# A hand-written order of single-engine steps, extended over all eight attention units and a second weight chunk

## The chip, the cores and the metric

The kernel runs on one core of a Trainium2 chip. The metric is device time in microseconds (us) of one execution. A core has a matrix engine (TensorE, "PE" in profile rows; its weight loads are "PEld"), VectorE ("DVE"), ScalarE ("ACT"), GpSimd ("POOL") and SyncE ("SP"), which issues most of the transfers. Each engine runs its own instructions in the order in which they stand and waits for the others by semaphores. That order is settled when the program is built.

## The reference

Attention with 32 packed queries per head, then two feed-forward layers over 2,304 tokens, all in float32:

```python
def sm_attn(qq, kk, vv):                        # scale = 1/8
    s = scale * np.matmul(qq, kk.transpose(0, 1, 3, 2))
    a = np.exp(s - np.max(s, axis=-1, keepdims=True))
    a = a / (np.sum(a, axis=-1, keepdims=True) + 1e-09)
    return np.matmul(a, vv)
p_packed = sm_attn(p, k, v)                     # q, k, v: 4 x 8 x 576 x 64, p: 4 x 8 x 32 x 64
x = sm_attn(q, p_packed, p_packed)              # then 2304 x 512
h = x @ w_in                                    # 512 x 2048
x = (np.maximum(h, 0) + np.log1p(np.exp(-np.abs(h)))) @ w_out
out = (1 / (1 + np.exp(-(x @ w_gate))) * (x @ w_val)) @ w_out2      # 512 x 1536, 1536 x 512
```

## The kernel before

**Attention** is cut into eight units `u = 2b + g`: batch `b` (of 4), a group `g` of four heads. The steps of a unit, each on one engine (class `Unit`; the two letters are their names in the list below):

- `lk`, `lq`, `lv`: SP loads k, q or v of the unit, 576 KB each, into a *place*. Places 0 to 5 are sixths of the tile `xa`, which later takes the first layer's output (batches 0 and 1 in 0 to 2, batches 2 and 3 in 3 to 5); place 6 is a tile of its own. A load into a place waits until what stood there has been read. `PLACE` (L216) gives the places of k, q and v of each unit.
- `kx`, `qx`: GpSimd (suffix p, L112) or ScalarE (a, L406) copies half of k or q into another order (tile `x`, two buffers); `kt`, `qt`: three transposes on TensorE (L416); `kc`, `qc`: ScalarE (a) or VectorE (d) takes them out of PSUM (L104, L106). `tp`, `cp`: the same for p (L384, L391).
- `sc` (L440): scores on TensorE; `mx`, `ex`, `nm`: maximum, exponential, division (VectorE, ScalarE, VectorE); `wt`, `wc`: the weights transposed (L472) and taken out; `va` (L492): the product with v, after which v's place is free; `pk`: the packed values into the tile `bdT`; `sp`: their split into two parts.
- `ss` (L521): the second scores, in two halves of the 576 tokens; `sb` (VectorE, L534 and L535), `ee` (ScalarE, L541), `sm` (VectorE, L545 to L547), `ml` (GpSimd, L551): their softmax; `tn` (L572): three transposes on TensorE; `hh`, `hl`: the result split into two parts, `A2h` and `A2l`.

**The first layer** goes by batch `b`, by chunk `c` of 256 of the 2,048 columns of `w_in`, and by half `s` of the tokens. `ri`, `ro` load raw weights (two buffers), `ci`, `co` convert them in three VectorE steps each, `oh`, `ol` split `w_out`. `wp` (L708) multiplies the packed values with `w_in`, `wh` and `wl` split the product; `hp` (L121 to L123, 12 matmuls) multiplies it with the attention weights; `ha` (three ScalarE steps), `hg` (VectorE), `gh` (ScalarE or GpSimd) and `gl` (GpSimd, L109) make the activation and split it; an `op` (L864, L865, L867, six matmuls) is a quarter `m` of the product with `w_out`, and `oc` adds it into `xa`. **The second layer** follows; the change doesn't touch it.

**The order.** `first_part` (L1075) walks through `SCRIPT` (L1047), a list of 371 words. Each word issues one of the steps; the digits are unit, head pair and half, or batch, chunk, half and quarter. `*n` puts n filler matmuls (L371) ahead of the step; there are 102 of them in all. While it runs, `held` keeps every engine's instructions in the order of the words. The list covers units 0 to 4 (`NU = 5`) and chunk 0 of batches 0 and 1. A loop over `entries` (batch, chunk) does the rest: for each it emits `hp` and the activation of this entry and the `op` of an earlier one, and between quarters it advances a queue of weight work (`jobs`) and, by a pace worked out from what is left, the attention units 5 to 7 (`attn_unit`, up to three alive at a time). Instructions of the loop are put in order by the tile framework's scheduler when the program is built.

```python
        for m in range(KD):
            take_out1(b, c, s, m, product_out1(c, m, g), CP0)
            between(m, att_ticks)
```

Of the kernel before, what the change touches and what calls it, by code (L numbers as in the profile page):

```python
# [21 lines left out]
def attn_moe_moe_kernel(  # L22
# [182 lines left out]
    def convert_split(key, pool, shape, tag, bufs):  # L205
# [61 lines left out]
    jobs = deque()  # L267
# [87 lines left out]
    E1 = nc.scalar  # L355
    WARM = 0
    BEHIND = []
    NU = 5
    FOUR = 3
    SPC = 2  # L360

# [660 lines left out]
    def prep_B(ps, f):  # L1022
# [22 lines left out]


    SCRIPT = """  # L1047
        lk0 lk1 lq0 lv0 lq1 lv1 tp0 cp0 kx00p tp1*7 kx01a cp1 lk2 kt000*12 kt001 ri00 kc000a
        kt010 kc001d kt011 kc010d kc011a kx10p tp2*5 sc0 kx11p kt100 mx0 cp2 kt101 kt110 kc100a
        qx01p kt111 kc110a kc101d ex0 kc111d qt010*10 qt011 sc1 qc010a nm0 qc011a qx00a mx1 wt01  # L1050
        wt00 lq2 qt000 wc00a wc01d qt001 ex1 qc000d va0*4 qx10p qc001a nm1 qx11p qt101 pk0a lv2
        qt100 qc101d qt110 ri01 sp0 ss01 qc100d lk3 qc110d wt10 sb01 ss00 wc10a qt111 ee01 sb00
        wt11 kx20p tp3 qc111a wc11a kx21p sm01 kt201*10 cp3 kt200 va1 ee00 ml01 ci000 kc200a
        ci001 kc201a kt211 pk1a kt210 sm00 tn01 kc211a sp1 ss10 kc210a ci002 qx20a sc2 ml00 sb10
        ro00 hh01 lq3 qt200 qx21p tn00 hl01 ee10 mx2 ss11*5 hh00 lv3 qc200a sm10 ex2 qt211 qt210
        hl00 qc211a ml10 sb11 qc210a qt201*12 qc201a ci010 tn10*11 ee11 nm2 hh10 kx31p tp4*7 cp4
        hl10 wt21*8 kx30p kt310 ci011 wc21a kt311 wt20 kc310a kt301 ci012 kc311a kt300 kc301a
        co000 ro01 wp00 kc300a sm11 wc20a sc3 wh00 co001 qx30p va2 qx31p mx3 ml11 co002 ex3
        qt301 lk4 qt311 wl00 oh00p lq4 pk2a lv4 qc311a nm3 tn11*11 sp2 ri10 ss20 qc301a hh11
        co010 wt30 ol00 sb20 wt31 wc30a hp000 wc31a hl11 ee20 co011 va3 ha000 sm20 qt310 co012  # L1060
        ml20 ss21 pk3a hg000 ri11 qc310a tn20 sp3 wp10 oh01a sb21 hh20 ss31 ol01 wh10 hl20 ee21
        wl10 qt300 hp001 kx40a kx41p sb31 qc300a gh000p sm21 kt401 ee31 kt411 gl000 kc401a ss30
        ci100 ha001 kc411d kt400 op0000 sb30 qx40p op0001 ml21 oc0000a hg001 op0003 kc400a
        oc0001d ee30 gh001p qt400 ci110 kt410 oc0003a qt401 ci111 qx41p qc400a op0002 kc410a
        sm30 gl001 tn21 qc401a qt410 oc0002a qt411 sc4 hh21 ci112 ml30 qc410a qc411a hl21 op0011
        sm31 tn30 oc0011a op0012 hh30 mx4 ml31 op0013 oc0012a hl30 ex4 op0010 ci101 tn31 oc0013a
        hp100 ci102 oc0010a hh31 nm4 ro10 wp01 ro11 ha100 hl31 wt41 wt40 wc41d hp101 wc40d wh01
        hg100 va4 wl01 ha101 gh100p co100 gl100 co101 hp010 pk4a co102 op1001 hg101 oh10p ha010
        op1000 co110 ol10 co111 ss41 gh101p co112 oc1001a op1003 oc1000a gl101 hg010 oh11a ss40
        oc1003a sb41 op1002 ol11 gh010a hp011 sb40 ee41 gl010 oc1002a sm41 ee40 op1013 ha011  # L1070
        sm40 ml41 op1011 op1012 oc1013d ml40 oc1011a op1010 hg011 sp4 oc1012a tn41 gh011a
        oc1010d tn40 hh40 gl011 hh41 hl40 hl41
    """

    def first_part():  # L1075
# [14 lines left out]
        for word in SCRIPT.split():  # L1090
# [18 lines left out]
            elif do in ("lk", "lq", "lv"):  # L1109
                assert place[do[1], at[0]] not in busy  # L1110
                load_one(do[1], at[0], place[do[1], at[0]])
            elif do in ("ri", "ro"):
                assert waiting[0] == ({"ri": "in", "ro": "out"}[do], *at)
                load_next()
            elif do == "ci":
                c, f, _ = at
                if (c, f) not in part:
                    if f == 0 or c not in w_in_f:
                        w_in_f[c] = ph1.tile([P, KD, CF], F32, tag="w_in", bufs=2, name="w_in")
                    part[c, f] = convert(("in", c, f), w_in_f[c][:, :, f * P : (f + 1) * P])  # L1120
                next(part[c, f], None)
            elif do == "co":
                if at[:2] not in raw_cv:
                    raw_cv[at[:2]] = new_cv()
                    part["o", *at[:2]] = convert(("out", *at[:2]), raw_cv[at[:2]])
                next(part["o", *at[:2]], None)
            elif do == "oh":
                wo_hl[at] = [
                    wo_p.tile([P, DM], F32R, tag="wo" + y, bufs=4, name="wo" + y) for y in "hl"
                ]  # L1130
                hi_of(eng != "p", wo_hl[at][0], raw_cv[at])
            elif do == "ol":
# [279 lines left out]
```

## Time and profile before

| | before |
|---|---|
| three runs | 858.75, 863.81, 864.49 us (median 863.81) |
| profiled execution | 858.43 us, of which the span from first to last instruction is 856.6 us |
| TensorE busy | 833.8 us, 97% of the span |
| VectorE, ScalarE, GpSimd busy | 595.9, 333.1, 497.6 us |
| mean granted TensorE clock | 0.998 |

In the profile "busy" counts instructions from start to modelled end, and matmuls overlap, so the time lost is better seen in the idle time ahead of an instruction and in what ended it. The clock column gives the share of full speed that was granted.

### The profile page before, as it was taken

The page shows a single profiled execution, that of the slowest core. Times are in us where ns is not written, and L with a number is a line of the kernel's source. Part 1 is how long each engine was busy: PE and PEld are TensorE (multiplying, and loading weights), DVE is VectorE, ACT ScalarE, POOL GpSimd, SP SyncE. Part 2 cuts the span into 40 slices and gives each one's busy share as a digit, 9 for nine tenths or more (in the row PEclk, how much of TensorE's full clock was granted, in tenths as well). Part 3 has the DMA queues.
Part 4 walks back from the last instruction along what each step waited for, and adds up shares of the span by engine and source line. Part 5 has one row for each costly group of instructions (what it writes and reads, how often), then busy time and mean ns, then how long its engine had stood idle before and what let it go on. Part 6 is the DMA issues. An engine that isn't in the chain of part 4 may idle for free.

```text
span 856.6 us, 15955 instructions
## 1 busy us (share of the span) xinstructions
PE 833.8 (97%) x6218; PEld 777.9 (91%) x6218; DVE 595.9 (70%) x1003; ACT 333.1 (39%) x615; POOL 497.6 (58%) x497
## 2 busy tenths in 40 slices
PE   9899989999999999999999999999999999999997
PEld 6789879999999999999999999999988999999995
DVE  4799456946746375458898688897896656766665
ACT  4677656554433334434324422232442432322210
POOL 4485434245857474693679787796892733536400
PEclk9999999999999999999999999999999999999999
DMA  9983330304453233500164464544414412213003
GB/s 230 219 219 103 84 84 2 99 1 121 128 152 106 69 99 99 154 2 1 42 194 152 138 192 151 168 140 155 142 56 142 125 44 80 68 44 111 14 1 111
DMA packets 61868, 90.83 MB, mean 106 GB/s; under 512 B 7648, under 2 KB 40544, under 8 KB 61792
## 3 DMA queue, kind: packets, MB, share of 16 engines
q1 hardware_dynamic: 60784, 88.56, 36.8%
q10 hardware_dynamic: 1008, 1.25, 0.4%
q8 instruction: 49, 0.80, 0.4%
q14 instruction: 27, 0.22, 0.1%
HBM read 65.67 MB, written 18.87 MB: 99 GB/s over the span
## 4 chain that ended last, share of the span: by engine, by line
PE 42%; DVE 5%; DMA 1%; issue 1%; ACT 1%; POOL 0%; DVEq 0%; ACTq 0%
PE bank L123 9%; PE bank L121 9%; PE bank L122 9%; PE ps L1327 5%; PE ps L1328 5%; PE ps L1329 5%; DVE aop L109 1%; DMA raw_v<-in_moe_w_val_dram 1%; DVE bank L1280 1%; DVE work L1280 1%; DVE work L1292 0%; DVE xa L1335 0%; DVE xa L903 0%; DVE sum L903 0%; ACT aop L929 0%
## 5 line engine op out<-in xcount | busy, mean ns | idle before, releaser
L121 PE MATMUL bank<-aop,BH 128*128 128x288 f32 x672 | 199.1, 296 | 3.7 <-DVE work L1292 0.9
L123 PE MATMUL bank<-aop,BL 128*128 128x288 f32 x672 | 198.6, 296 | 0.0
L122 PE MATMUL bank<-aop,BH 128*128 128x288 f32 x672 | 197.8, 294 | 0.2 <-DVE aop L109 0.2
L875 DVE TENSOR_TENSOR xa<-xa,ps 128x288 f32<-128x288 f32 x224 | 99.5, 451 | 101.0 <-PE ps L867 100.8
L109 POOL TENSOR_TENSOR ghl<-g,ghl 128x576 fp32r<-128x576 f32 x64 | 93.4, 1463 | 101.4 <-ACT ghl L116 76.6
L864 PE MATMUL ps<-ghl,woh 128*128 128x288 f32 x512 | 146.4, 301 | 3.2 <-DVE xa L875 2.2
L865 PE MATMUL ps<-ghl,wol 128*128 128x288 f32 x512 | 143.5, 295 | 0.0
L121 PEld LDWEIGHTS bank<-aop,BH 128*128 128x128 f32 x672 | 126.2, 188 | 9.6 <-POOL BL L109 1.1
L122 PEld LDWEIGHTS bank<-aop,BH 128*128 128x128 f32 x672 | 126.4, 188 | 4.1 <-DVE aop L109 0.4
L123 PEld LDWEIGHTS bank<-aop,BL 128*128 128x128 f32 x672 | 126.5, 188 | 0.0
L109 POOL TENSOR_TENSOR BL<-cv,BH 128x512 fp32r<-128x512 f32 (+1 forms) x96 | 117.3, 1237 | 3.4 <-ACT BH L116 2.4
L867 PE MATMUL ps<-ghl,woh 128*128 128x288 f32 x512 | 109.3, 295 | 0.1
L864 PEld LDWEIGHTS ps<-ghl,woh 128*128 128x128 f32 x512 | 96.1, 188 | 6.7 <-DVE xa L875 3.2
L865 PEld LDWEIGHTS ps<-ghl,wol 128*128 128x128 f32 x512 | 96.3, 188 | 0.1
L1280 DVE TENSOR_TENSOR work<-work,bank 128x576 f32<-128x576 f32 (+1 forms) x100 | 70.8, 725 | 31.1 <-PE bank L123 31.0
L1327 PE MATMUL ps<-oh,gv 128*128 128x512 f32 x216 | 84.5, 391 | 1.0 <-DVE xa L1335 0.6
L1328 PE MATMUL ps<-ol,gv 128*128 128x512 f32 x216 | 84.9, 393 | 0.0
L1329 PE MATMUL ps<-oh,gv 128*128 128x512 f32 x216 | 84.8, 393 | 0.0
L867 PEld LDWEIGHTS ps<-ghl,woh 128*128 128x128 f32 x512 | 82.3, 188 | 0.7 <-POOL ghl L109 0.6
L112 POOL TENSOR_SCALAR BH<-cv 128x512 fp32r<-128x512 f32 (+1 forms) x48 | 30.1, 638 | 89.0 <-PE bank L122 88.8
L1335 DVE TENSOR_TENSOR xa<-xa,ps 128x512 f32<-128x512 f32 x90 | 61.6, 684 | 28.2 <-PE ps L1329 27.9
L121 PE MATMUL ps<-A2h,wph 128*128 128x288 f32 x256 | 76.6, 299 | 0.1
(151 smaller groups left out, 1645.1 us busy)
## 6 DMA issues: line engine op xcount, KB each, us to landing
cv<-B SPq DMA_DIRECT2D x52, 256.0 KB, 2.7
B<-cv SPq DMA_DIRECT2D x48, 256.0 KB, 3.6
raw_in<-in_moe_w_in_dram SPq DMA_DIRECT2D x16, 512.0 KB, 3.9
raw_out<-in_moe_w_out_dram SPq DMA_DIRECT2D x16, 512.0 KB, 3.6
raw_g<-in_moe_w_gate_dram SPq DMA_DIRECT2D x12, 512.0 KB, 3.9
raw_v<-in_moe_w_val_dram SPq DMA_DIRECT2D x12, 512.0 KB, 4.3
raw_o<-in_moe_w_out_dram SPq DMA_DIRECT2D x12, 512.0 KB, 4.2
xs<-cv SPq DMA_DIRECT2D x56, 64.0 KB, 2.0
```

The costliest lines, as they stand in the source:

```text
L109: hold(eng.tensor_tensor(lo, x, hi.bitcast(F32), op=ALU.subtract))
L121: hold(nc.tensor.matmul(ps, wh, xh, start=first, stop=False))
L122: hold(nc.tensor.matmul(ps, wh, xl, start=False, stop=False))
L123: hold(nc.tensor.matmul(ps, wl, xh, start=False, stop=last))
L864: hold(nc.tensor.matmul(out_, wh[:, ms], gh[:, f], start=f == 0, stop=False))
L865: hold(nc.tensor.matmul(out_, wl[:, ms], gh[:, f], start=False, stop=False))
L867: hold(nc.tensor.matmul(out_, wo_hl[c, f][0][:, ms], gl[:, f], start=False, stop=f == 1))
L875: hold(nc.vector.tensor_tensor(dst, dst, out_, op=ALU.add))
L1280: nc.vector.tensor_tensor(to, x, y, op=ALU.add)
L1327: nc.tensor.matmul(bank, gh[:, ts_], oh, start=f == 0, stop=False)
L1328: nc.tensor.matmul(bank, gh[:, ts_], ol, start=False, stop=False)
L1329: nc.tensor.matmul(bank, gl[:, ts_], oh, start=False, stop=f == 1)
```

## The change

`SCRIPT` grows from 371 to 585 words. It goes on over units 5 to 7 and over chunk 0 of batch 2 (up to its activation) and chunk 1 of batches 0 and 1, and it is arranged anew from its first line on; the number of fillers stays 102. `NU` is 8, so no unit is left to the loop, and the loop begins two entries later. Units 6 and 7 get places of their own. Some copies change engines: in the stretch that differs VectorE has nine instructions more, ScalarE seven and GpSimd two fewer. No operation of the computation is added or removed. From unit 7's last transposes (`tn`) on, TensorE's instructions stand in the same order in both kernels to the end; ahead of it they are the same ones in another order.

```diff
     PLACE = {
         0: "345", 1: "621", 2: "345", 3: "634", 4: "563", 5: "456",
-        6: "565", 7: "656",
+        6: "345", 7: "634",
     }
...
-    NU = 5
+    NU = 8
...
     SCRIPT = """
-        lk0 lk1 lq0 lv0 lq1 lv1 tp0 cp0 kx00p tp1*7 kx01a cp1 lk2 kt000*12 kt001 ri00 kc000a
+        lk0 lk1 lq0 lv0 lq1 lv1 tp0 cp0 kx00p kx01a kt010*24 lk2 kt000 ri00 kc010d kt001 kc000a
...
-        oc1010d tn40 hh40 gl011 hh41 hl40 hl41
+        hl40 tn41 qt510 oc0113 hh41 va5 kx60p kx61a hl41 qc510a kt611 pk5a lk7 kt610 kc611d
+        kt601 lq7 sp5 kc610a ss50 kc601d qx60a op0100 sb50 kt600 op0101 qx61p kc600a oc0100 ee50
...
+        tn71 hh61 hl70 hh71 hl61 hl71
     """
...
             elif do == "ci":
                 c, f, _ = at
                 if (c, f) not in part:
-                    if f == 0 or c not in w_in_f:
+                    if c not in w_in_f:
...
-        for b, c in ((0, 0), (1, 0)):
+        for b, c in ((0, 0), (1, 0), (0, 1), (1, 1)):
             for s in range(2):
                 gt.pop((b, c, s))
...
-    jobs.append(("wp11", prep_wp_one(1, 1)))
+    jobs.append(("wp21", prep_wp_one(2, 1)))
...
-    pend.extend((0, 1, s) for s in range(2))
+    pend.extend((2, 0, s) for s in range(2))
     for i, (b, c) in enumerate(entries):
-        if i < 3:
+        if i < 5:
             continue
```

What this does to the engines' orders, at two places. The first is TensorE around unit 5's second softmax. Before, the loop's order has unit 6's scores (`L440`) and four groups of k or q transposes, then both of unit 5's `tn` (`L572`, reading its tiles `a2`) and two `wp`:

```order
L440 MATMUL ps2_1676<-kT_1574,pT0_109 64x288 x4
L416 MATMUL ps1_1695<-ident_101,x_1693 128x96 x3
L416 MATMUL ps1_1701<-ident_101,x_1693 128x96 x3
L416 MATMUL ps1_1708<-ident_101,x_1706 128x96 x3
L416 MATMUL ps1_1713<-ident_101,x_1706 128x96 x3
L572 MATMUL ps1_1720<-ident_101,a2_1644 128x96 x3
L572 MATMUL ps1_1726<-ident_101,a2_1660 128x96 x3
L708 MATMUL ps1_1732<-w_in_462,bdT_106 64x256 x4
L708 MATMUL ps1_1741<-w_in_947,bdT_106 64x256 x4
L121 MATMUL ps2_1750<-A2h2_116,wph_1737 128x288
```

In the changed kernel the first of the two (`tn50`) stands behind a `wp` and the first transposes of unit 7's k (`kt711`, `kt710`):

```order
L708 MATMUL ps1_1632<-w_in_466,bdT_106 64x256 x4
L416 MATMUL ps1_1640<-ident_101,x_1630 128x96 x3
L416 MATMUL ps1_1647<-ident_101,x_1630 128x96 x3
L572 MATMUL ps1_1651<-ident_101,a2_1577 128x96 x3
L440 MATMUL ps2_1657<-kT_1547,pT0_109 64x288 x4
L416 MATMUL ps1_1665<-ident_101,x_1638 128x96 x3
L121 MATMUL ps2_1674<-A2h2_116,wph_1644 128x288
```

and the second (`tn51`) comes 47 rows later, behind an `hp` (its last row stands first here) and unit 6's `ss61`, with `va7` and unit 6's first `tn` after it:

```order
L123 MATMUL ps2_1832<-A2h1_115,wpl_1814 128x288
L521 MATMUL ps1_1850<-bdT_106,qT_1606 96x64 x6
L572 MATMUL ps1_1864<-ident_101,a2_1724 128x96 x3
L492 MATMUL ps1_1868<-a1T_1827,xa_78 64x32 x24
L572 MATMUL ps1_1902<-ident_101,a2_1846 128x96 x3
L416 MATMUL ps1_1906<-ident_101,x_1699 128x96 x3
```

So the two `tn` of the unit no longer stand together, and each has other products ahead of it. The second place is SP's queue with the loads of the last units. Before, chunk 2's raw weights are followed by k6, v6, q6, k7, v7, q7 (those named `xa_78` are in a place of `xa`):

```order
L165 DMA raw_in_1382<-in_moe_w_in_dram 128x4x256
L165 DMA raw_in_1384<-in_moe_w_in_dram 128x4x256
L252 DMA xa_78<-in_k_dram 96x4x384
L252 DMA xa_78<-in_v_dram 96x4x384
L252 DMA q6_1606<-in_q_dram 96x4x384
L252 DMA k7_1718<-in_k_dram 96x4x384
L252 DMA v7_1864<-in_v_dram 96x4x384
L252 DMA xa_78<-in_q_dram 96x4x384
```

In the changed kernel k6, p7, q6 and v6 stand ahead of those weights, and k7, q7, v7 behind them:

```order
L252 DMA xa_78<-in_k_dram 96x4x384
L311 DMA p_1257<-in_p_dram 128x64 x2
L252 DMA xa_78<-in_q_dram 96x4x384
L252 DMA xa_78<-in_v_dram 96x4x384
L165 DMA raw_in_2085<-in_moe_w_in_dram 128x4x256
L165 DMA raw_in_2087<-in_moe_w_in_dram 128x4x256
L252 DMA k7_1541<-in_k_dram 96x4x384
L252 DMA xa_78<-in_q_dram 96x4x384
L252 DMA xa_78<-in_v_dram 96x4x384
```

The three loads of unit 7 now follow one another, and k7 is the one in place 6.

## Rows read from the trace of the kernel before

**Rows 1.** The page's first part: busy us (share) xinstructions.

```profile
span 856.6 us, 15955 instructions
PE 833.8 (97%) x6218; PEld 777.9 (91%) x6218; DVE 595.9 (70%) x1003; ACT 333.1 (39%) x615; POOL 497.6 (58%) x497
```

**Rows 2.** Busy time by stretch: from:to, length, each engine's busy us, granted clock, DMA share, GB/s.

```profile
1.50:45.00 43.50, 39.64 (x488) 31.69 (x489) 26.16 (x64) 23.45 (x64) 20.61 (x32) 1.00 1.01 235
45.00:60.00 15.00, 15.00 (x173) 14.04 (x172) 13.95 (x26) 12.23 (x27) 11.39 (x16) 1.00 0.95 234
60.00:90.00 30.00, 28.77 (x263) 26.05 (x262) 25.84 (x47) 19.02 (x41) 18.91 (x20) 1.00 0.32 93
90.00:120.00 30.00, 26.88 (x244) 22.08 (x243) 15.05 (x34) 17.79 (x44) 12.08 (x16) 0.94 0.40 100
120.00:151.00 31.00, 29.93 (x322) 28.06 (x321) 18.65 (x46) 18.09 (x43) 11.67 (x17) 1.00 0.08 21
0.00:151.00 151.00, 140.28 (x1480) 121.97 (x1481) 100.13 (x216) 91.35 (x218) 75.61 (x106) 0.99 0.55 134
151.00:857.00 706.00, 693.49 (x4740) 655.96 (x4738) 495.75 (x787) 241.76 (x399) 421.99 (x391) 1.00 0.34 100
```

**Rows 3.** TensorE's timeline: start, us, what, count [idle before <-what ended it].

```profile
35.58 0.30 PE L384 MATMUL ps<-ident,p 128*128 128x128 f32 x1 [2.44 <-DMA p<-in_p_dram]
...
42.33 0.47 PE L416 MATMUL ps<-ident,x 96*128 96x96 f32 x3 [0.56 <-POOL x L112]
42.63 0.78 PE L371 MATMUL ps<-hot 128*128 128x128 bf16 x11
...
64.02 0.47 PE L572 MATMUL ps<-ident,a 96*128 96x96 f32 x3 [1.18 <-POOL a L551]
...
109.17 1.51 PE L416 MATMUL ps<-ident,x 96*128 96x96 f32 x12 [0.17 <-POOL x L112]
111.75 0.47 PE L572 MATMUL ps<-ident,a 96*128 96x96 f32 x3 [1.07 <-POOL a L551]
113.00 0.74 PE L572 MATMUL ps<-ident,a 96*128 96x96 f32 x3 [0.79 <-POOL a L551]
...
150.17 0.47 PE L572 MATMUL ps<-ident,a 96*128 96x96 f32 x3 [0.85 <-POOL a L551]
```

**Rows 4.** TensorE's timeline, sixteen `wp` instructions at two places.

```profile
113.68 3.25 PE L708 MATMUL ps<-w_in,bdT 128*64 128x256 f32 x16
...
151.38 1.95 PE L708 MATMUL ps<-w_in,bdT 128*64 128x256 f32 x16
```

**Rows 5.** GpSimd's timeline, the copies of unit 3's k.

```profile
35.11 1.63 POOL L112 TENSOR_SCALAR x<-k 96x768 f32<-96x768 f32 x2 [3.86 <-DMA k<-in_k_dram]
```

**Rows 6.** Timelines of TensorE and GpSimd: unit 5's second scores and softmax multiplies.

```profile
104.86 2.18 PE L521 MATMUL ps<-bdT,qT 128*96 128x64 f32 x24
...
110.86 0.83 POOL L551 TENSOR_TENSOR a<-a,m 96x384 f32<-96x384 f32 x1 [0.96 <-ACT qT L104]
112.12 0.83 POOL L551 TENSOR_TENSOR a<-a,m 96x384 f32<-96x384 f32 x1 [0.43 <-ACT a L456]
```

**Rows 7.** Loads of k1, k3, k7 (tile `k`) to landing; ScalarE's copies of k or q.

```profile
DMA to landing us min/median/max: 4.4/5.7/16.0
...
L406 ACT ACTIVATE x<-xa 96x768 f32<-96x768 f32 x4 | 3.4, 840 | 0.4 <-DMA xa<-in_q_dram 0.4
```

**Rows 8.** TensorE's timeline: the first matmuls of two `op` that follow each other.

```profile
82.18 0.29 PE L864 MATMUL ps<-ghl,woh 128*128 128x288 f32 x1
...
82.99 0.29 PE L864 MATMUL ps<-ghl,woh 128*128 128x288 f32 x1
```

**Rows 9.** Groups by line in 0:151: VectorE's copies of k's transposes (busy us, mean ns).

```profile
L106 DVE COPY kT<-ps 128x288 f32<-128x288 f32 x5 | 2.1, 451 | 7.4 <-PE ps L416 7.4
```

**Rows 10.** Waits in 0:151: total us, times, longest.

```profile
PE ps L572 <- POOL a L551: 3.9, 4, 1.2
```

More of the change, by code (lines that the diff above doesn't have):

```diff
@@ L1047, in attn_moe_moe_kernel @@
     SCRIPT = """
-        lk0 lk1 lq0 lv0 lq1 lv1 tp0 cp0 kx00p tp1*7 kx01a cp1 lk2 kt000*12 kt001 ri00 kc000a
[L1049 to L1070, printed above, removed]
@@ L1071, in attn_moe_moe_kernel @@
-        sm40 ml41 op1011 op1012 oc1013d ml40 oc1011a op1010 hg011 sp4 oc1012a tn41 gh011a
-        oc1010d tn40 hh40 gl011 hh41 hl40 hl41
+        lk0 lk1 lq0 lv0 lq1 lv1 tp0 cp0 kx00p kx01a kt010*24 lk2 kt000 ri00 kc010d kt001 kc000a
+        kt011 kc001d tp1 kc011a kx10p cp1 sc0 kx11p tp2 kt100 mx0 cp2 kt101 kt111 kc100a kt110
+        qx01p kc101d ex0 kc110d qx00p qt010*12 kc111a nm0 qt011 sc1 qc011a lq2 qc010d wt01 mx1
+        wt00 wc01a qt000 qt001 wc00a ex1 va0*6 qx11p qc001a nm1 qx10p qc000a qt110 pk0a lv2
@@ new lines, in attn_moe_moe_kernel @@
+        qt111 ri01 qt100 qc110a sp0 qc111d ss01 lk3 qc100d wt11 sb01 ss00 wc11a wt10 ee01 sb00
+        qt101 kx20p wc10a qc101a va1*9 sm01 kx21p ee00 sm00 ml01 kt200 pk1a kt210 ci000 tn01
+        kc200a sp1 kt201 ci001 kc210a kt211 kc201a ss10 ci002 kc211a qx21p hh01 sc2 sb10 ro00
+        ml00 lq3 hl01 ee10 qx20p mx2 qt210*11 tn00 qc210a lv3 qt200 sm10 hh00 tp3 qt201 ex2 hl00
+        ml10 ci010 cp3 ss11*14 ci011 qc200a qc201a tn10 qt211 nm2 hh10 qc211a sb11 wt20*13 kx30p
+        kx31a hl10 wc20a kt300*13 ci012 ee11 kt311 tp4 kt310 kc300a co000 ro01 kc311a wt21 sm11
@@ new lines, in attn_moe_moe_kernel @@
+        cp4 kt301 kc310a wp00 kc301a co001 ml11 wc21a sc3 qx30a co002 qx31p va2 wh00 mx3 oh00a
+        wl00 ex3 ol00 qt311 lk4 qt310 pk2d tn11 lq4 qc311a nm3 ss21 lv4 sp2 hh11 ri10 qc310a
+        qt300 hl11 wt31 sb21 qc300a wt30 hp000 wc31a wc30a co010 ee21 co011 va3 ha000 sm21 co012
+        ml21 tp5 ss20 pk3a hg000 ri11 cp5 sp3 tn21 lk5 wp10 oh01a sb20 hh21 ss30 ol01 wh10 hl21
+        ee20 wl10 qt301 hp001 qx40p kx40a sb30 qc301a gh000p sm20 ee30 qt401 gl000 kt401 qc401a
+        qt400 kt400 kc401d ha001 ss31 kc400d qx41p qc400d op0002 sb31 kx41p qt411 oc0002a op0001
@@ new lines, in attn_moe_moe_kernel @@
+        hg001 ml20 qc411a op0000 ee31 ci110 gh001p oc0001a kt411 ci111 op0003 oc0000a gl001
+        kc411a ci112 kt410 oc0003a qt410 tn20 kc410a sm31 kx51p op0012 qc410a hh20 op0011 sm30
+        ml31 oc0012a kx50a tp6 sc4 hl20 ml30 oc0011a ci100 kt501 ci101 cp6 op0013 kc501a mx4
+        kt500 oc0013a tn30 op0010 hh30 kc500d ex4 hl30 kt511 tn31 ci102 hp100 hh31 oc0010a nm4
+        ro10 kc511a ro11 wp01 lq5 ha100 hl31 lv5 wt41 wt40 wc41d kt510 hp101 kc510d wh01 hg100
+        wc40a wl01 gh100p sc5 ha101 co100 gl100 co101 va4 mx5 op1003 pk4a lk6 hg101 lq6 ex5
@@ new lines, in attn_moe_moe_kernel @@
+        op1002 sp4 co110 co111 ss40 oc1003a qx51p qx50a co112 hp011 oc1002a lv6 sb40 oh11p qt511
+        gh101p ha011 op1000 nm5 gl101 qt500 qt501 co102 hp010 qc511a qc501d oh10p oc1000a hg011
+        qc500a op1011 ol10 ha010 op1013 oc1011d ol11 wt50 oc1013d tp7 op1010 wc50d cp7 ss41
+        hg010 gh011a oc1010a gl011 op1012 sb41 ee40 wt51 oc1012a op1001 sm40 ee41 op0110 gh010p
+        wc51a sm41 oc1001a op0111 ml40 op0112 oc0110 ml41 oc0111 tn40 oc0112 op0113 gl010 hh40
+        hl40 tn41 qt510 oc0113 hh41 va5 kx60p kx61a hl41 qc510a kt611 pk5a lk7 kt610 kc611d
@@ new lines, in attn_moe_moe_kernel @@
+        kt601 lq7 sp5 kc610a ss50 kc601d qx60a op0100 sb50 kt600 op0101 qx61p kc600a oc0100 ee50
+        qt601 oc0101 qt600 lv7 qc601a qt611 sm50 qt610 qc600a op0102 qc610a qc611d ml50 kx71a
+        wp20 oc0102 kx70p kt711 wh20 kt710 tn50 qx71p sc6 wl20 hh50 hl50 kt700 kc710a mx6 hp200
+        kc700a kc711a ex6 kt701 qt710 qx70p kc701a ss51 nm6 ha200 sc7 qc710d sb51 wt60 wt61
+        wc60a qt701 mx7 qt711 wc61a op0103 qc701a hg200 va6 ex7 oc0103 gh200p qc711a nm7 gl200
+        ee51 wp11 pk6a sm51 wt70 sp6 wh11 wt71 ss60 wc70a wl11 wc71a ml51 hp111 sb60 ee60 ss61
@@ L1073, in attn_moe_moe_kernel @@
+        ha111 sm60 tn51 va7 sb61 ml60 hh51 hg111 ee61 tn60 qt700 hl51 pk7a hp110 qc700d gh111a
+        sp7 sm61 hh60 ss70 ha110 hl60 ml61 ss71 sb70 gl111 hp201 hg110 ee70 sm70 gh110a op1111
+        ha201 sb71 ml70 op1112 op1110 gl110 oc1111 oc1112 op1113 ee71 hg201 op1101 oc1110 gh201p
+        op1100 oc1113 gl201 sm71 op1102 oc1101 op1103 ml71 oc1100 tn70 oc1102 tn61 hh70 oc1103
+        tn71 hh61 hl70 hh71 hl61 hl71
     """
```

## The prediction

> **What bounds the kernel now.** I read the page's first part, then busy time by stretch, then TensorE's timeline with the idle time ahead of each row. The page says TensorE is busy 97% of the span [rows 1]; the other engines matter only where TensorE waits for them. The order shows where the change can act: from the piece `tn71` (unit 7's last turning, 150.17 us in the trace [rows 3]) to the end, TensorE has the same instructions in the same order in both kernels, and ahead of it the same instructions, 102 fillers among them, in another order. So the stretch 0 to 151 us is in play and the 706 us behind it are not. In 0:151 TensorE is idle 151.00 − 140.28 = 10.72 us [rows 2]. By stage: 3.86 in 1.5:45, nothing in 45:60, 1.23 in 60:90, 3.12 in 90:120 and 1.07 in 120:151 [rows 2]; the rest is the first 1.5 us.
>
> The list of before ends with unit 4's last pieces, ahead of the stretch 90:120; from there on the loop interleaves units 5 to 7. So the list's own stretch from 45 to 90 loses 1.23 us and the loop's from 90 to 151 loses 4.19. The clock comes on top: in 90:120 the granted clock is 0.94 on average [rows 2], all else being 1.00, so TensorE dropped to its lower level (1.2 of 2.4 GHz) for a while. What it did before: twelve transposes, a wait of 1.07 us, three transposes, a wait of 0.79, three transposes [rows 3]. The same sixteen `L708` products then took 3.25 us, and 1.95 at full clock [rows 4]: 1.3 us lost at least; 0.06 of 30 us is 1.8 at most. I take 1.5.
>
> **The change part by part.**
>
> *The late waits (removed).* Two of the three largest waits of 90:151 are unit 5's turnings `tn` and the third is unit 7's, all for the GpSimd multiply that ends the softmax [rows 3]. In before both halves of unit 5's second product run back to back (104.86 to 107.04) and the multiplies end at 110.86 + 0.83 = 111.69 and 112.95 [rows 6]: the chain needs 4.7 us for the first half and 5.9 for the second. The loop put too little between. In after's order, behind `ss50` stand three `op`, seven transposing words and a `wp` ahead of `tn50`: 3 × 0.81 [rows 8] + 7 × 0.38 (1.51 / 4 for three transposes [rows 3]) + 1.95 / 2 [rows 4] = 6.1 us, against 4.7. Behind `ss51` stand a whole `hp` (12 matmuls of 0.81 / 6, 1.6 us), two `ss` (2.18 [rows 6]), two transposing words (0.76), a `va` and four `wt` ahead of `tn51`: 4.5 us before the last two kinds are counted, and the half runs alone, so 4.7 is its chain. Behind `ss71` stand an `hp` and eight `op`, 1.6 + 6.5 = 8.1 us, against 5.9. So I expect these waits gone, and with them the clock's fall: 4.19 + 1.5 = **5.7 us**. Bounds: 3.1 (only the three waits that I traced, 1.07 + 0.79 + 0.85, and 0.4 of the rest) and 4.19 + 1.8 = 6.0.
>
> *The start (rearranged).* Unit 3's k arrives when the loads let it: its first copy on GpSimd begins at 35.11, the moment of landing [rows 5], since the queue is full (DMA share 1.01 up to 45 us [rows 2]). SP's queue is the same in both orders up to unit 5's k, so I leave that time alone. Before waits 2.44 us at `tp4` [rows 3] and afterwards still runs 19 of its 102 fillers; after has run all 102 by then, and one `wt` more, but has `tp4` yet to do. Eleven fillers take 0.78 us at most [rows 3], so 19 are up to 1.35 us that after has spent inside an unavoidable wait; some of before's lie inside waits too (eight while the copy finishes). I take **0.95**; bounds 0 and 1.7 (19 fillers and a `wt`, three transposes, of 0.38).
>
> *Unit 7's own places (added).* k7 goes to place 6, which v5 holds until `va5` has read it; q7 follows in place 3, v7 in 4. k7's load is issued behind `va5`, and TensorE wants the copy of k7 at `kt711`. Between stand eight transposing words, an `ss` and three `op`: 8 × 0.38 + 1.09 + 3 × 0.81 = 6.6 us, less where a row's end lies beside the next one's start; I take 5.4. The load takes 4.4 us with an empty queue [rows 7] and the ACT copy 0.84 [rows 7], 5.4 with handovers: a wait of 0 to 0.8, **0.3** taken. Everything behind `kt711` on TensorE waits with it. Ahead of k7 on SP stand two weight loads (chunk 2) that wait for `co102`; an `hp`, nine `op` (1.6 + 7.3 us) and small pieces stand between `co102` and `va5`, so they should be out of the way.
>
> *Copies moved between engines.* In the changed stretch VectorE gets nine instructions more, ScalarE seven fewer, GpSimd two fewer. Nine copies of 0.45 [rows 9] are 4.1 us on an engine that is busy 100.13 of 151 [rows 2]: cost nothing, hidden in its 51 us of idle time. Where it is fullest, 25.84 of 30 in 60:90 [rows 2], the cover is 4.2 us; if all nine fell there, up to 4.1 would show. After spreads chunk 1's weight conversion over a longer list, which relieves that spot. I take 0.
>
> *Waits that the longer list brings.* From below nothing; from above the rate of before's own list, 1.23 us in 45:90, over the 61 us of the replaced stretch: 1.7. I take **0.5** beside k7's 0.3, since the three chains above have cover. The waits of 45:90 I leave as they are.
>
> Sum: 5.7 + 0.95 − 0.3 − 0.5 = 5.85 us. The profiled execution took 858.43 (a span of 856.6 and 1.8 around it), so **852.6** for an execution like it. That execution is 5.4 below the median of the three runs shown (863.81); the four executions (858.43, 858.75, 863.81, 864.49) have a mean of 861.4, 2.9 above it. The trace doesn't show what makes the longer ones; I expect the changed kernel to scatter alike and add 2.9: **855.5**.
>
> **The rivals** (times as for the profiled execution; 0 to 5.4 comes on top of each).
>
> *The waits only move.* The list is fixed on every engine, and GpSimd runs a split of an activation ahead of a softmax multiply wherever the list says so; 64.02 shows such a wait inside before's list, 1.18 us [rows 3]. Five of that size among the eight `tn` of units 4 to 7 cancel the gain: 858.4. For it: the list of before has one. Against: one in 45 us, and the covers worked out above. Decides from the fifth on. The same time comes out if the common 706 us give the lead back: TensorE is idle only 706 − 693.49 = 12.5 us there [rows 2], so a part could be held by loads or by VectorE; against it, SP's queue brings chunk 2's weights no later in after.
>
> *Unit 7's loads hold TensorE: slower.* k3 took 16.0 us from issue to landing in a full queue [rows 7]. If k7 met such a queue (chunk 2's weights and v6 still going), `kt711` would wait 16.0 + 0.84 − 5.4 = 11.4 us and the time would be 852.6 + 11.1 = 863.7. It is slower than before from a landing of some 10.8 us on. Against it: the DMA share is 0.40 in 90:120 and 0.08 in 120:151 [rows 2], so the queue should be short.
>
> *The clock falls more often.* Each fall costs 1.3 to 1.8 us [rows 4]. The list puts units 6 and 7 closely together, from `va5` to `hp200` with three `op` as the only large products. Four falls cancel the gain: 852.6 + 4 × 1.5 = 858.6; one or two give 854 to 855.6. Against it: in 1.5:45 nearly all of TensorE's work is transposes and small products, and the granted clock is 1.00 throughout, with a wait of 2.44 us in it [rows 2, 3]. The Trainium skill, "TensorE: Matmul & The Clock Gate", section "Part 4: PE-mode transpose", says that transposes don't count as a busy TensorE for the clock; by that rule this rival would be the likeliest, and the start would run at the lower level, which the trace contradicts.
>
> **How the numbers follow.** The forecast 0.64 (849.7 to 855.5 as profiled; with the scatter 849 to 860); waits that only move 0.20 (856 to 860, with scatter to 865); unit 7's loads 0.07; the clock 0.09. The low end: all waits behind 45 us, the wait of 0.56 at 42.33 [rows 3], the clock and the start at their best, 1.23 + 4.19 + 0.56 + 1.8 + 0.95 = 8.7, so 849.7. The range 849 to 862 leaves out the upper half of the second case and most of the third. One per cent, 8.6 us, is about what a measurement of this kernel can tell from no change. Faster by more needs the best of every term, or a scatter that the change ends: 0.17. Slower by more needs unit 7's loads and another case: 0.06. Within: 0.77.
>
> **What would show it.** Right: TensorE's last `L572` starts near 144 us instead of 150; the granted clock is 1.00 from 90 to 151; `L572`'s waits for GpSimd's `L551` fall from 3.9 us [rows 10] to under 1.5; idle time in the first 145 us is near 6. Wrong: a wait of `L416` for a copy of k7 above 1 us (the loads), a stretch below 1.00 (the clock), or the last `L572` at 144 with a span that is no shorter (given back behind).

## The result, and the profile after

| | before | after |
|---|---|---|
| median | 861.16 us (858.31 to 867.9, 8 executions) | 850.97 us (849.06 to 856.64, 8 executions) |
| ratio | | 0.9879, 95% interval 0.9843 to 0.9915 |
| profiled execution | 858.43 us, span 856.6 | 851.06 us, span 849.3 |

The changed kernel is faster by 1.2%, or 10.2 us, in this comparison, and by 7.7 us (0.9%) when both kernels ran once more (e1 below). The range of the prediction (849 to 862) holds the time; its point, 855.5, is 4.5 us too high. Its likeliest case, within 1%, did not come here and came by a little in e1; both intervals hold the line at 1%. The profiled execution gained 7.4 us. One execution of the kernel before beside e9 to e12 took 909.64 us in a slower state, at a mean clock of 0.846, and stands outside the ratios.

The page's first part of the changed kernel, which answers to [rows 1]:

```profile
span 849.3 us, 15970 instructions
PE 832.6 (98%) x6218; PEld 779.3 (92%) x6218; DVE 601.6 (71%) x1012; ACT 333.2 (39%) x608; POOL 496.5 (58%) x495
```

Busy time by stretch of the changed kernel (from:to, length, each engine's busy us, granted clock, DMA share, GB/s), which answers to [rows 2]:

```profile
1.50:45.00 43.50, 40.78 (x471) 32.39 (x471) 25.56 (x58) 22.95 (x63) 21.14 (x29) 0.92 0.91 220
45.00:60.00 15.00, 14.74 (x174) 13.74 (x173) 13.39 (x30) 12.10 (x28) 10.05 (x16) 1.00 0.93 238
60.00:90.00 30.00, 29.45 (x276) 26.77 (x275) 26.33 (x48) 21.97 (x50) 17.61 (x19) 1.00 0.70 171
90.00:120.00 30.00, 29.84 (x357) 26.70 (x356) 21.58 (x52) 19.44 (x45) 14.78 (x23) 1.00 0.26 62
120.00:151.00 31.00, 30.45 (x262) 28.36 (x259) 23.99 (x51) 17.55 (x32) 11.54 (x14) 1.00 0.02 2
151.00:849.00 698.00, 687.30 (x4695) 651.28 (x4694) 490.30 (x777) 238.39 (x394) 420.48 (x390) 1.00 0.35 101
```

TensorE's idle time in 90:120 fell from 3.12 us to 0.16, and the clock there rose from 0.94 to 1.00. In 120:151 it fell from 1.07 to 0.55, in 60:90 from 1.23 to 0.55; in 45:60 it rose from nothing to 0.26. Against that, the clock in 1.5:45 fell from 1.00 to 0.92.

To see where the time went I cut the span at two matmuls that both kernels have: the first of the first `hp` (`hp000`), and the first of the `hp` of batch 3, chunk 0, from which on TensorE's order is the same in both (the common part). TensorE's timelines at these places, before and then after:

```profile
45.07 0.38 PE L121 MATMUL ps<-A2h,wph 128*128 128x288 f32 x1
...
153.26 0.40 PE L121 MATMUL ps<-A2h,wph 128*128 128x288 f32 x1
```

```profile
47.37 0.38 PE L121 MATMUL ps<-A2h,wph 128*128 128x288 f32 x1
...
146.62 0.40 PE L121 MATMUL ps<-A2h,wph 128*128 128x288 f32 x1
```

| us | before | after | after, another execution (e1 below) |
|---|---|---|---|
| up to the first `hp` | 45.07 | 47.37 | 45.38 |
| from there to the common part | 108.19 | 99.25 | 99.43 |
| common part | 703.3 | 702.7 | 702.7 |
| span | 856.6 | 849.3 | 847.5 |

So the list's stretch gained 8.8 to 8.9 us, the start lost 0.3 to 2.3, and the common part neither held the lead back nor added to it beyond 0.6.

**A correction.** The sections ahead of the prediction, and the prediction, say that from unit 7's last turning (`tn71`) on TensorE has the same order in both kernels. That was misread. In the changed kernel `tn71` is the end of this row, and some 10 us of the loop's products follow before the order becomes the same, with an `op`:

```profile
132.86 1.17 PE L572 MATMUL ps<-ident,a 96*128 96x96 f32 x9
...
143.86 0.29 PE L864 MATMUL ps<-ghl,woh 128*128 128x288 f32 x1
```

Before, that `op` stands right behind the last `tn` [rows 3]:

```profile
150.42 0.38 PE L864 MATMUL ps<-ghl,woh 128*128 128x288 f32 x1
```

So the cut at 151 us was right for the kernel before and the sum did not suffer, but the sign "last `L572` near 144" could not come true. The cuts of the table lie one `op` and sixteen `wp` products (2.8 us) into the same order.

### The profile page after: what moved, and what is told of

Its sections match the earlier page's. It is cut to its first block, busy times and chain, and to the rows that moved or that the text cites. A ratio compares the mean times of both kernels' runs of the same rounds, so it can differ in the third digit from the quotient of the medians.

```text
span 849.3 us, 15970 instructions
## 1 busy us (share of the span) xinstructions
PE 832.6 (98%) x6218; PEld 779.3 (92%) x6218; DVE 601.6 (71%) x1012; ACT 333.2 (39%) x608; POOL 496.5 (58%) x495
## 5 line engine op out<-in xcount | busy, mean ns | idle before, releaser
L1294 DVE TENSOR_TENSOR bank<-work,bank 128x576 f32<-128x576 f32 (+1 forms) x75 | 54.7, 736 | 31.9 <-PE bank L123 31.7
```

The lines of the kernel that those rows point to most:

```text
L1294: nc.vector.tensor_tensor(to, x, y, op=ALU.add)
```

## The experiments

All are kernels run beside the kernel before on the same chip. "To the common part" and "from the first `hp`" are the cuts of the table above, read from the profiled execution of each kernel.

**The changed kernel and the kernel before once more.** No edit; e1 is the changed kernel and e5 the kernel before.

> The changed kernel as it is, beside the three kernels that share this chip. If its gain lies in the stretch from the first large product (hp000) on, its ratio to before is 0.988 again, hp000 starts some 2 us later than before's 45.1 us, and the last softmax turning (tn71) some 16 us earlier than before's 150.2. If the clock's fall between 26.7 and 33.5 us of its profiled execution belongs to its start, it shows again (a loss of about 3.4 us of full clock); if it is chance, it is absent or elsewhere.

> The kernel before as it is, for a second profile of it. If the stalls of its loop stretch are fixed by its order, the same waits of L572 for L551 stand at unit 5's and unit 7's turnings, and hp000 starts within 0.5 us of 45.1 unless the clock falls earlier. If the falls of the clock are chance, one may stand at another place than 113 us, or none. Ratio 1.00.

e1: 850.16 us against 857.84, ratio 0.9917 (0.9889 to 0.9945). e5: 856.7 against 858.13, ratio 0.9985 (0.9953 to 1.0017). So the gain is there again, 7.7 us of it, and the kernel against itself shows no difference. The profiled execution of e5 has the waits of [rows 3] at unit 5's `tn` again, and the clock falls behind them again:

```profile
113.28 0.47 PE L572 MATMUL ps<-ident,a 96*128 96x96 f32 x3 [1.07 <-POOL a L551]
114.54 0.74 PE L572 MATMUL ps<-ident,a 96*128 96x96 f32 x3 [0.79 <-POOL a L551]
...
90.00:120.00 30.00, 26.87 (x236) 21.66 (x235) 14.87 (x35) 16.83 (x42) 12.19 (x17) 0.90 0.35 86
```

In e10 (below), which has this order too, both waits and the fall are there as well. So the waits belong to the order; the fall came in all three profiles, though single executions of before with a mean clock of 1.000 can't have had it.

In the profiled execution of e1 the granted clock is 1.00 in the start, too:

```profile
1.50:45.00 43.50, 39.00 (x488) 31.50 (x489) 27.32 (x64) 23.73 (x66) 23.19 (x33) 1.00 1.01 229
```

The 0.92 of the first profile is therefore a matter of the single execution. There the clock fell to its lower level (1.2 of 2.4 GHz) between 26 and 33 us; this is the profiled execution of the changed kernel again:

```profile
24.00:26.00 2.00, 1.53 (x26) 1.12 (x23) 1.42 (x6) 1.25 (x4) 1.96 (x4) 1.00 1.09 243
26.00:30.00 4.00, 4.00 (x27) 3.40 (x28) 2.61 (x5) 1.12 (x3) 3.31 (x6) 0.54 1.09 265
30.00:33.00 3.00, 3.00 (x23) 2.14 (x20) 2.25 (x7) 0.59 (x2) 0.77 (x1) 0.50 1.09 290
33.00:36.00 3.00, 2.06 (x28) 1.96 (x28) 2.13 (x6) 2.49 (x8) 1.87 (x2) 0.98 1.10 249
```

Just ahead of the fall TensorE was busy for 1.53 of 2 us. The fall cost about 1.8 us: the first `hp` came 2.0 us later than in e1, the common part 1.8.

**One half of the change alone.** e6 keeps units 5 to 7 in the list, with their new places, and leaves chunk 1 of batches 0 and 1 and batch 2 to the loop. e7 keeps chunk 1 in the list, except the eight `op` of batch 1, and leaves these, units 5 to 7 (with their old places, `NU` is 5) and batch 2 to the loop. In both the words that stay keep their order, and the loop begins correspondingly earlier.

```diff
 # e6 against the changed kernel; SCRIPT without the words of chunk 1 and batch 2 that before's lacks; cut to one place
-        for b, c in ((0, 0), (1, 0), (0, 1), (1, 1)):
+        for b, c in ((0, 0), (1, 0)):
...
 # e7 against the changed kernel; SCRIPT without the words of units 5 to 7, of batch 2 and of op11; cut to two places
-    NU = 8
+    NU = 5
-        for b, c in ((0, 0), (1, 0), (0, 1), (1, 1)):
+        for b, c in ((0, 0), (1, 0), (0, 1)):
```

> The changed kernel's list with all eight units, but without the products that it adds (chunk 1 of batch 1 and the op of chunk 1 of batch 0, batch 2's first product); these are left to the loop, which starts at the same entry as before's. Theory A, the gain comes from large products standing between the steps of units 5 to 7: they are gone here (four hp and twelve op, 16 us of cover), so TensorE waits 6 us or more for the softmax steps of units 5 to 7 and the clock falls at least once: 858 us or more, no gain. Theory B, it is enough that the units stand in the list instead of the loop: 851.

> The other half: the list with chunk 1's products as in the changed kernel, but units 5 to 7 left to the loop (with the places of before), which now has only the last eight op of batch 1 and the first products of batch 2 beside them. Theory A: the units have still less beside them than in before, so L572 and the transposes wait longer, 862 us or more. Theory B, chunk 1 in the list is what gains: 853.

Both are slower than before by about 1%: e6 took 869.6 us (ratio 1.0107, 1.0041 to 1.0174), e7 867.6 (1.0088, 1.0058 to 1.0118). From the first `hp` to the common part they need 118.4 and 116.8 us, where the whole change needs 99.4 and before 108.2. Busy time by stretch, e6 and then e7:

```profile
90.00:120.00 30.00, 25.16 (x294) 21.10 (x295) 15.67 (x42) 14.53 (x38) 12.23 (x24) 0.79 0.27 61
120.00:151.00 31.00, 27.53 (x188) 24.64 (x188) 15.31 (x34) 14.11 (x23) 6.61 (x6) 0.82 0.00 1
```

```profile
90.00:120.00 30.00, 23.33 (x185) 19.11 (x186) 10.55 (x25) 15.90 (x41) 11.68 (x16) 0.73 0.32 80
120.00:151.00 31.00, 30.80 (x313) 27.23 (x311) 15.38 (x36) 16.98 (x39) 10.27 (x16) 0.93 0.16 39
```

In e6 TensorE is idle for 8.3 us in these 61 and runs at a clock of 0.79 and 0.82; in e7 it is idle for 6.9, at 0.73 and 0.93. The clock can take more than the waits: its missing share times the length of the stretches makes up to 11.9 us in e6 and 10.3 in e7 (an estimate). What it waited for between 45 and 165 us, e6 and then e7 (sum, times, longest):

```profile
PE ps L572 <- POOL a L551: 6.6, 5, 2.0
PE ps L416 <- ACT x L406: 1.2, 1, 1.2
PE ps L472 <- ACT bdT L104: 0.9, 1, 0.9
```

```profile
PE ps L472 <- DVE a L465: 3.6, 1, 3.6
PE ps L572 <- POOL a L551: 1.6, 3, 0.9
```

Without the large products of chunk 1 between them, five of the `tn` of the last units wait for GpSimd's multiply. Without the units between them, the units that the loop still has to do wait for their own chains. So what gains is the mixture: each half is the cover of the other, and neither the longer list as such nor the places alone do it. Both runs leave words out and arrange nothing anew; that no order of one half could gain is not shown, and neither is what the new places are worth in the whole change.

**Unit 5's two halves together again.** In the list, the words of the second half of unit 5's softmax stand right behind those of the first:

```diff
-... ss50 kc601d qx60a op0100 sb50 ... ml50 ... tn50 ... ss51 nm6 ... tn51
+... ss50 ss51 kc601d qx60a op0100 sb50 sb51 ... ml50 ml51 ... tn50 tn51
```

> One place of the changed kernel put back as before had it: unit 5's second half (ss51 to hl51) stands directly behind its first half's steps, so that tn50 and tn51 stand together behind some 5.4 us of TensorE's work, where the second multiply needs 5.9 us from the end of ss51. Theory A (cover too short): tn51 waits for L551, 0.5 to 1.5 us with what is hidden under the row before it, and 851 to 852 us beside 850.2 (plus 1.5 if the clock falls). Theory B (the cover there doesn't matter): no wait and 850.

850.65 us, ratio 0.9883 (0.9819 to 0.9947), which is the time of the changed kernel. From the first `hp` to the common part it takes 100.35 us, 0.9 more than e1, a size that only the trace shows. The second `tn` does wait, but not for its multiply, which had ended at 102.19; it waits for VectorE's split of a `wp` that ended later:

```profile
102.91 0.44 PE L572 MATMUL ps<-ident,a 96*128 96x96 f32 x3 [0.44 <-DVE wpl L109]
```

The waits named in the prediction for unit 5 were thus worth little singly once there is other work around them; it is the sum of all places that counts.

**Something else was in e8's profile.** Its span is 5 us longer than e1's though it entered the common part at the same time (144.85 and 144.81). VectorE's timeline of e8, then of e1, at the same place, one of the instructions of `fold_A`, which adds two quarters of `xa`:

```profile
442.50 4.69 DVE L903 TENSOR_TENSOR xa<-xa 128x576 f32<-128x576 f32 x1
```

```profile
442.54 0.87 DVE L903 TENSOR_TENSOR xa<-xa 128x576 f32<-128x576 f32 x1
```

GpSimd's timeline of e8 in these microseconds:

```profile
441.63 1.31 POOL L109 TENSOR_TENSOR BL<-cv,BH 128x512 fp32r<-128x512 f32 x1
442.88 0.64 POOL L112 TENSOR_SCALAR BH<-cv 128x512 fp32r<-128x512 f32 x1
443.47 0.64 POOL L112 TENSOR_SCALAR oh<-cv 128x512 fp32r<-128x512 f32 x1
444.05 1.31 POOL L109 TENSOR_TENSOR BL<-cv,BH 128x512 fp32r<-128x512 f32 x1
445.30 1.28 POOL L109 TENSOR_TENSOR ol<-cv,oh 128x512 fp32r<-128x512 f32 x1
```

VectorE's addition began while GpSimd was at work and ended only when GpSimd's unbroken run of instructions was over, at 446.58. In e1 it was GpSimd's next instruction that took longer, 1.13 us instead of 0.64:

```profile
442.76 1.13 POOL L112 TENSOR_SCALAR BH<-cv 128x512 fp32r<-128x512 f32 x1
```

TensorE's wait for VectorE there, e8 and then e1, and the stretch behind it in e8:

```profile
PE bank L121 <- DVE work L1304: 4.6, 1, 4.6
...
450.00:460.00 10.00, 10.00 (x63) 9.91 (x64) 8.12 (x13) 2.39 (x4) 9.90 (x12) 0.83 0.41 130
```

```profile
PE bank L121 <- DVE work L1306: 0.9, 1, 0.9
```

That is 3.7 us of wait more, and 1.7 us of clock (0.17 of 10): the 5 us. The profiles of e6, e7 and e9 (below) have the same wait of 4.6 us, so 5 us of their spans are not their edits' own; the figures from the first `hp` to the common part are free of it. Of the twelve profiles with this fold on VectorE these four have the hold. The Trainium skill, "SBUF — State Buffer", section "Who interferes with whom", says that a VectorE instruction with two inputs in SBUF contends with a GpSimd instruction that reads SBUF, and that the order of issue decides who blocks. The rows agree that one blocks the other; they go further than the page, which speaks of the length of one instruction: here four went past. What decides between the two outcomes stays open: the addition began 0.43 us before the end of a GpSimd instruction in e8 and 0.26 in e1, but 0.60 in e3, where it took only 1.22 us.

**The fold on the other engine.** To see whether this is what makes some executions 5 us longer, the four instructions of `fold_A` went to GpSimd, where they can't run beside its own work:

```diff
-        tt(x21, x21, x22, ALU.add)
+        nc.gpsimd.tensor_tensor(x21, x21, x22, op=ALU.add)
...
-        tt(x21, x21, x11, ALU.subtract)
+        nc.gpsimd.tensor_tensor(x21, x21, x11, op=ALU.subtract)
```

> The changed kernel with the four instructions of fold_A (L908, L910) on GpSimd instead of VectorE. In one kernel's execution VectorE's xa<-xa at 442.50 took 4.69 us, as long as GpSimd ran without a pause, TensorE waited 4.6 us and the clock fell; in others it took 0.87 at the same place. Theory (that hold makes executions 5 us longer, in either kernel, by chance of 0.2 us): with the fold on GpSimd no execution is 4 us above the fastest, all lie between 847 and 850, and the median is 849 or less. Rival (the scatter has another cause): the times still fall into two groups 4 to 5 us apart, or GpSimd's 5 us of added work (four of about 1.3 us) make TensorE wait for it and the median is 851 or more.

849.25 us, 847.84 to 849.62, ratio 0.9904 (0.9883 to 0.9925); all five executions lie within 1.8 us, and GpSimd's added work costs nothing that can be seen. The median is 0.25 above what the theory wanted. It is what the theory says, but five executions don't settle how often the hold comes: of the changed kernel's first eight, seven lie within 3.7 us as well. The hold itself is shown; its share in the scatter is not. The scatter of the kernel before is mostly another thing: of 17 executions on e1's chip, the eight with a mean granted clock of 0.997 or more took 855.0 to 858.1 us, the three of 0.993 or less 861.1 to 866.9.

**The start and the fillers.** e2 puts before's words up to the first `hp` in front of the new list, and what these lack of the new start right behind; e3 moves 26 of the 102 fillers ahead; e4 leaves all of them out of the changed kernel, e10 out of the kernel before, and e12 does e4's edit and the fold's.

```diff
 # e3
-tn01 ... ss10 ... wt20*13 ... kt300*13
+tn01*13 ... ss10*13 ... wt20 ... kt300
 # e4, e10 and e12: every "*n" left out
-qt010*12 ... va0*6 ... va1*9 ...
+qt010 ... va0 ... va1 ...
```

> The changed kernel with the words up to hp000 in before's order and everything behind in the new order. Theory A, the start lost and the rest of the list won: hp000 at 45 us instead of 47.4, the rest of the new list as fast as in the changed kernel, 2 us faster than it: 849 us as profiled, ratio 0.986. Theory B, the new start is no slower in itself and only met a fall of the clock by chance: the same time as the changed kernel within 0.1%, apart from executions in which the clock falls.

> The changed kernel with the 26 fillers of wt20 and kt300 (which sit ahead of the wait for unit 3's k) moved to tn01 and ss10, some 10 us earlier, ahead of where the clock fell. Theory A, the clock fell because TensorE had little but small products and waits there: the fall from 26.7 to 33.5 goes, and hp000 comes at 45 to 46 us instead of 47.4; 849 us, ratio 0.986. Theory B, the place of the fillers doesn't matter and the loads alone set that stretch: hp000 at 47.4 and the time is the same, 851.

> The changed kernel without any of the 102 fillers of the list (they take part in no result). Fillers take 0.056 us each, 5.7 us in all. If they only fill waits for loads, taking them away changes nothing as long as the clock holds: 851. If half of them lie outside waits, 2 to 3 us are saved: 848.5. If they hold the clock, it falls once or more in the first 45 us, at 1.5 to 3.4 us each: 852 to 856.

> The kernel before without its 102 fillers (matmuls whose results nobody reads). Without them the changed kernel took 848.75 instead of 850.16. Theory (fillers only cost time, 0.07 us each where they don't fall into a wait, and don't hold the clock): 1 to 1.5 us less than before, so 856.6 to 857.1, and the changed list is worth the same 8 us with and without fillers. Rival (before needs them, since it waits 2.44 us at 35.58 and the work around it is transposes): the granted clock falls more often or longer in the first 60 us, and the time is 859 to 862.

> Both edits in the changed kernel: no fillers, and fold_A on GpSimd. If the two causes are independent: the changed kernel without fillers (848.75, some executions longer) less its longer executions, so 847.5 to 848.5, the fastest of all. If the fold on GpSimd costs time there: 849 or more.

e2: 854.71 us, 0.9964 (0.9932 to 0.9995), so some 4.5 us of the gain are lost. It reaches the first `hp` at 43.6 us, 1.8 earlier than e1, but the new list behind it counts on what the new start has already done: in the old start `ss20` stands ahead of the first `hp`, in the new one `ss21`, so in e2 the softmax behind `ss21` begins later, and `tn21` waits for its multiply. Its timeline and the stretch:

```profile
50.85 0.74 PE L572 MATMUL ps<-ident,a 96*128 96x96 f32 x3 [1.56 <-POOL a L551]
...
45.00:60.00 15.00, 13.04 (x131) 11.22 (x130) 8.34 (x18) 9.31 (x20) 7.41 (x11) 0.77 0.73 180
```

The two waits of 1.96 us in all (the other is 0.40) and the clock of 0.77 that follows put the common part at 148.3 us instead of 144.8. So the list behind rests on what the new start has done by then, and the two can't be priced apart by the first `hp`. What the old start would be worth with a list that fits it, e2 doesn't show.

e3: 849.3 us, 0.991 (0.9877 to 0.9943), the same as e1; in its profile the clock still falls near 25 us, for 3.4 us, so the place of these fillers doesn't stop it. e4: 848.75, 0.9896 (0.9873 to 0.9919), 1.4 less than e1 with intervals that overlap. Its start runs at a lower clock:

```profile
1.50:45.00 43.50, 37.54 (x379) 28.20 (x380) 25.60 (x63) 24.14 (x65) 22.60 (x32) 0.88 0.93 224
```

and still its first `hp` comes at 46.0 and the common part at 145.3. e10: 859.23 us, 1.002 (0.9993 to 1.0047): before neither gains nor loses by leaving them out beyond the noise. Its executions have mean clocks of 0.989 to 0.996, those of the kernel before beside them 0.992 to 1.000. In all three profiles without fillers (e4, e10, e12) the clock falls in the first 45 us, in the eleven with them in three (the changed kernel's first, e3 and e5). So the fillers do hold the clock up, and in both kernels they cost about what they save; the theory that they only cost and the rival that before needs them are both too strong. e12: 848.45, 0.9914 (0.9883 to 0.9944), with one execution at 853.93 that has no fold on VectorE but a mean clock of 0.992. No version beats the changed kernel by more than the measurement can tell.

**Unit 7's k later.** The load of k7 goes behind that of v7 on SP's queue.

```diff
-... va5 ... kt611 pk5a lk7 kt610 kc611d ... qt610 qc600a op0102
+... va5 ... kt611 pk5a kt610 kc611d ... qt610 qc600a lk7 op0102
```

> The changed kernel with one word moved: the load of unit 7's k is issued behind the load of its v instead of ahead of its q's. In the changed kernel that load was issued at 96.61 us, landed 4.7 us later, the ScalarE copy ended at 102.58 and TensorE's kt711 began at 103.17 without a wait, so its cover is some 0.6 us. Moved, it should be issued near 101 us and land near 105.7, with kt711 at about 107.1. Theory (place 6 and the load behind it are the next bound, with hardly any cover): TensorE waits 3.5 to 4 us for the copy of k7, and the time rises from 850.2 to 853.5 to 854. Rival (something else has the same slack, or what follows makes the lead up): a wait that is shown, but the first product of batch 3 begins as before, near 145 us, and the time is 850 to 851.

In e1 (timelines of ScalarE and TensorE) the copy of k7 ends 0.6 us (100.77 against 101.35) ahead of the transposes that need it:

```profile
99.94 0.83 ACT L406 ACTIVATE x<-k 96x768 f32<-96x768 f32 x1
...
101.35 0.71 PE L416 MATMUL ps<-ident,x 96*128 96x96 f32 x6
```

and in e9, with the two stretches behind:

```profile
106.34 0.84 ACT L406 ACTIVATE x<-k 96x768 f32<-96x768 f32 x1 [6.02 <-DMA k<-in_k_dram]
...
107.24 1.22 PE L416 MATMUL ps<-ident,x 96*128 96x96 f32 x6 [5.52 <-ACT x L406]
...
107.00:110.00 3.00, 2.76 (x15) 2.06 (x17) 1.15 (x2) 1.08 (x3) 1.09 (x2) 0.50 0.02 5
110.00:113.00 3.00, 3.00 (x15) 2.13 (x12) 0.91 (x2) 1.65 (x5) 0.00 (x0) 0.50 0.01 3
```

856.59 us, 0.9992 (0.9967 to 1.0018): the whole gain is gone: by the two ratios e9 lies 6.4 us above e1, where I had expected 853.5 to 854, at most 3.8 above. The time of the transposes was right (107.24), the price wasn't, for two reasons. I had counted from the first profile, in which TensorE came to this place at 103.17, held up by the clock at the start; in e1 it is there at 101.35. The load was issued 4.6 us later (99.45 against 94.81) and took 6.8 us instead of 4.8; v7's, issued 0.4 ahead, ran beside it, and in e1 the load of q7, issued 0.4 behind that of k7, took 6.7. So TensorE waited 5.5. And behind the wait the clock stood at 0.50 for 6.8 us, which is another 3.4. From the first `hp` to the common part e9 takes 108.85 us, 9.4 more than e1. This profiled execution is the slowest of e9's ten (862.97 us, with the fold's hold in it), so the 9.4 is more than the usual price.

## Why the prediction was right or wrong

**What bounds the kernel: right.** All of the gain lies ahead of the common part, and there are no late transfers or other engines behind it that took it back (703.3 and 702.7 us).

**The late waits, 5.7 us: right as a mechanism, too small.** [rows 3]'s waits of unit 5's and 7's `tn` are gone, and [rows 10]'s sum of 3.9 us in four waits is now this row of TensorE's waits in the changed kernel:

```profile
PE ps L572 <- POOL a L551: 0.3, 1, 0.3
```

The stretch gained 8.8 us, where the prediction's terms for it (5.7 − 0.3 − 0.5) make 4.9. The step that failed is taking the idle time of the windows for the time lost. A row's end is modelled, and in these rows it lies later than the start of the next, so idle time begins to count too late. In TensorE's timeline of the changed kernel:

```profile
84.15 0.29 PE L121 MATMUL ps<-A2h,wph 128*128 128x288 f32 x1
84.29 0.29 PE L122 MATMUL ps<-A2l,wph 128*128 128x288 f32 x1
84.41 0.29 PE L123 MATMUL ps<-A2h,wpl 128*128 128x288 f32 x1
85.06 0.37 PE L864 MATMUL ps<-ghl,woh 128*128 128x288 f32 x1 [0.36 <-DVE qT L106]
```

The matmuls follow each other at 0.13 us, so the last could have begun at 84.54; it began 0.52 later, and 0.36 of that is shown. Measured so, from start to start, TensorE lost 8.67 us between the first `hp` and the common part of the kernel before, in 29 places, of which 5.41 shows as idle; in e1 it is 1.9, of which 0.88 shows. (This is my estimate from the timeline's rows: every start that came more than about 0.1 us later than is usual behind such a row.) The difference is 6.8 us of stalls. With the clock's fall in 90:120, 1.5 to 1.8 us as the prediction had it, it makes 8.3 to 8.6 of the 8.8. A smaller part of the miss, within the 6.8, is the stretch 60:90, which I left as it was and which lost 0.7 us less.

**The start, 0.95 us gained: wrong.** It came 0.3 us later in e1, and 2.3 in the profiled execution, where the clock fell. The new order has one more group of three transposes ahead of the first `hp`, 0.38 us by the prediction's own price, which makes up the 0.3. The fillers were the wrong term: leaving all 102 out changes the time by no more than the noise (1.4 us less in e4, 1.8 more in e10), and without them some of the clock goes. And e2 shows that the start can't be summed apart from the list, which rests on what the new start has done.

**Unit 7's k, 0.3 us: right within its bounds.** No wait at all; the load took 4.7 us, as in an empty queue. The count of what stands ahead of `kt711` left out `wp20`, eight products that take one us, and the cover that was there is 0.6 us: with the count as it was made there would have been none. So the wait is missing in part by luck. That the place is tight was right, and e9 shows that a wait there costs the clock behind it as well.

**Waits that the longer list brings, 0.5 us: about right**; 0.88 us of idle time, or 1.9 from start to start, are left in the stretch in e1, old and new together, so the term by itself is not measured. **The copies moved to VectorE: right**; it is busy 26.33 of 30 us in 60:90 against 25.84, and no wait of TensorE for it there is longer than the 0.36 us shown above.

**The rivals.** That the waits only move is refuted for the whole change, yet it is just what happens in e6 and e7, with a half of it. That unit 7's loads hold TensorE is refuted, and e9 is what it would have looked like: not slower than before, but equal. That the clock falls more often came true in a part: in the stretch that the rival spoke of there was no fall, and in the start it fell in some executions. The prediction held the start against the rule on transposes of the Trainium skill, "TensorE: Matmul & The Clock Gate", section "Part 4: PE-mode transpose". That went too far: of TensorE's 39 us in before's first 45 some 14 are transposes (an estimate from start to start of its rows) and the rest are products and fillers, so a clock of 1.00 there doesn't contradict the rule. No run here tests it. The same instructions ran there at 1.00 in e1 and at 0.92 in the first profile.

**The scatter, 2.9 us: wrong for the changed kernel.** Of the 4.5 us between 855.5 and 850.97, the sum accounts for 1.5 (852.6 against 851.06 for the profiled execution) and the scatter for the rest. Before's median of eight lies 2.7 us above its profiled execution, as assumed; after's lies where its profiled execution does. On the chips of the later runs before's median is 856.7 to 858.1, so the 2.9 belongs to the first executions more than to the kernel. The chance of faster by over 1%, 0.17, was given to the best of every term together; with the stalls read from start to start it would have been larger.

## What to carry to other kernels

The idle time that this profile shows ahead of matmuls is a lower bound of what a wait costs: compare starts with the usual distance of such rows, and add the clock behind a longer wait. Where two kinds of work cover each other, bring both into the same order; here one kind alone, in the order made for both, was worse than a loop that mixes them badly. Where a step has half a microsecond of cover, treat its transfer as fixed: a load issued 4.6 us later cost 6.4 us by the medians, and 9.4 in the profiled execution.

## What the runs showed of the hardware

- A VectorE addition with both inputs in SBUF took 4.69 us (e8) instead of 0.87 (e1), through four of GpSimd's instructions in a row; where it took 0.87, GpSimd's next instruction took 1.13 us instead of 0.64. What decides between the two is open.
- The same instructions ran at a granted clock of 0.92 in one execution and 1.00 in another (1.5 to 45 us); behind a wait of 5.5 us (e9) it stood at 0.50 from 107 to 113 us, and in the stretch with a wait of 1.6 us (e2, 45 to 60 us) it was 0.77 on average.
- Matmul rows of 0.29 us start 0.13 us apart, an overlap of 0.16 us, and the wait shown above at 85.06 comes out that much too short (0.36 instead of 0.52).
